# Transposes through the 128 rows of TensorE, or through its two 64-row halves: an RWKV-7 and SwiGLU kernel

## The chip, the core and the metric

The kernel runs on one core of a Trainium2 chip. The metric is the device time of one execution in microseconds (us), as the median of several runs. A profile of one execution tells what every engine did: TensorE (PE for matmuls, PEld for the loading of their stationary operand), VectorE (DVE), ScalarE (ACT), GpSimd (POOL) and SyncE (SP, which here only issues DMAs).

## What is computed

Two blocks follow each other. The first is a linear recurrence over 768 tokens for 4 x 8 heads of width 40, the second a feed-forward block on the 3072 rows of width 320 that the first one leaves.

```
for t in range(S):
    y[:, :, t] = einsum('bhd,bhde->bhe', r_t, state)
    Sa = einsum('bhde,bhe->bhd', state, a_t)
    state = state * w_t - outer(Sa, b_t) + outer(v_t, k_t)
...
x  = y as (batch*token, head*width)            # 3072 x 320
xn = x / sqrt(mean(x*x) + 1e-6) * g
out = (silu(xn @ w_gate) * (xn @ w_val)) @ w_out   # d_ff 1536
```

All data are fp32.

## The kernel before

**Tiling.** The 768 tokens are cut into 24 chunks of C = 32. The 32 pairs of batch and head lie as n (8), i (2, the half of 64 partitions in which the pair's tokens lie) and o (2, one of two heads that stand side by side). `front(c)` (L654) loads a chunk's inputs, transposes them, and builds the products of the decays and the triangular matrices by levels 4, 8 and 16; `inverse(c)` (L762; `early_inverse`, L780, for the first four) inverts a unit triangular matrix by 31 steps on VectorE; `main(c)` (L812) carries the state over the chunk and makes y; after each second chunk `feed(g)` (L941) runs the feed-forward block on 256 rows, in 12 slices of d_ff. The fronts run two chunks ahead of the mains.

**Natural tiles.** DMAs bring inputs with the tokens on partitions: a tile such as `wan` is [128, 8, 2, 64], where rows 0 to 63 belong to i = 0 and rows 64 to 127 to i = 1, and each head's 40 values stand in a slot of 64. Most matmuls need the head's width on partitions, so the kernel transposes such tiles on TensorE with an identity as the moving operand. All of these go through `flip` (L490, L491). One step of `plan` is a burst of flips, all into one room of PSUM:

- `turned` (L632 to L636) makes 8 flips, one for each n. In the front: `wan` (w and a, L670) and `kbn` (k and b, L684) with 128 rows and 104 columns of weights and 128 moving columns; `K` (L758) with 104 rows, 128 columns and 104 moving columns. In the main: `rn` (r, each second chunk, L847), `VU` (L856, out to `vut`) and the state `ST` (L860, out to `Sd`, 104 rows, 104 columns, 104 moving).
- `turn4` (L921) transposes y by 4 flips of 128 x 128, `turn3` (L932) the normalised x by 3.

After each burst ScalarE copies the room into SBUF: `T`, `A` and `Ab` (L678 to L682) from that of `wan`, `K` (L684), `KN` (L758), `rE` and `r2` (L849 to L852), `vut` (L856), `Sd` (L859); the Square and the scaling of `x` read that of y (L924, L927), and `xg` is made from that of x on ScalarE (chunks 0 to 5, L937) or VectorE (L939).

**Matmul shapes.** A matmul is told here by weights (rows x columns) and moving columns. The feed-forward block uses the whole array, 128*128, except for the last 64 rows of its 320 inputs: `h64` (L959) runs pairs with 64*128 weights, one in each half of the rows and each into another PSUM bank. The recurrence uses small ones: `gramk` (L693, L716) 40*64, `score` (L863) 40*64, `level` (L884) 128*40, `state`, `lower` and `update` 40*32, 32*32 and 64*40, and `y0` (L902) 40*40. Each fp32 matmul stands in the trace as two records, each transpose as one.

**Order.** Nothing is ordered by dependence at run time: `ORDER` (L33 to L228) lists all 6028 steps in the order in which they are issued, over all engines, each number counted from the first step that has not been issued; each "-" (151 of them) is a matmul on the identity that fills time (`plan.warm`, L1017). An engine works through its own steps in that order and waits by semaphores. PSUM is three rooms of two banks (`plan.pairs`, L439) and `po` for the feed-forward output; `PAIRS` (L230) says which of the three each step's output gets, and a room is held until its last reader is through.

Of the kernel before, what the change touches and what calls it, by code (L numbers as in the profile page):

```python
# [17 lines left out]
P = 128  # L18
C = 32
# [14 lines left out]
85 84 76 83 58 78 73 86 74 59 60 75 5 89 61 88 53 77 80 4 43 6 201 7 87 90 44 8 334 62 9 - - - - - - - - 93 10 18 79  # L34
11 12 214 557 13 213 567 14 15 94 566 210 16 17 95 558 108 200 - - - 97 96 19 335 20 21 2 209 22 23 98 25 199 568 26
100 578 202 24 101 107 569 111 57 - - - - - 102 106 124 589 27 122 112 392 109 103 52 119 113 104 54 577 155 125 110
204 105 120 - - - - - - 114 203 117 121 559 211 598 118 46 131 129 132 45 562 560 212 597 563 588 561 394 123 115 136
586 384 133 134 - - - - - 126 130 116 47 564 3 145 383 135 336 128 137 48 144 143 141 587 219 142 51 570 127 565 146
138 337 55 573 1005 216 579 281 393 220 582 608 571 390 234 379 239 607 572 583 580 380 251 574 222 38 221 609 575 581
42 - - - - - - - - 223 82 226 339 91 64 227 338 39 81 139 224 263 576 238 153 56 249 247 590 206 584 228 382 237 591  # L40
272 593 40 233 232 585 381 154 148 594 33 140 205 229 592 389 235 250 28 248 - - 325 236 32 245 36 230 147 260 282 391
246 259 150 35 34 326 595 0 36 270 155 214 148 242 243 62 605 598 230 - 239 40 616 599 601 628 64 49 91 600 602 30 48
626 1135 28 257 603 29 241 68 150 255 65 0 1347 194 0 194 84 173 0 - - - 182 540 200 0 557 184 1 186 935 542 540 0 506
515 527 257 513 300 0 111 97 110 61 112 96 51 439 458 122 50 243 480 0 244 0 58 255 242 0 259 709 104 120 246 708 247
456 470 258 488 719 0 256 470 457 242 0 716 265 487 104 0 268 0 0 265 473 0 262 277 0 273 0 236 0 260 0 269 0 461 241
- - - - - - - 237 242 0 0 278 242 243 252 0 252 0 0 89 0 99 246 0 97 0 230 94 440 0 230 94 440 231 - - - - - - - - -
240 441 244 0 0 468 440 451 255 0 42 468 269 469 258 215 440 239 204 0 0 257 253 203 93 449 92 212 0 235 - - - - - - -
- 246 0 437 0 262 0 246 247 436 245 464 470 258 259 469 260 244 - - 255 471 465 468 466 0 215 466 269 256 445 697 255
478 686 93 94 264 95 687 270 96 266 97 0 97 470 695 2 98 99 3 100 471 101 473 1 102 0 468 99 470 100 471 101 441 102
103 258 104 105 260 106 - - - - - - - - - - - 0 504 106 107 473 108 0 108 502 0 108 109 469 110 111 0 0 0 0 0 - - 13 0  # L50
374 16 146 143 14 147 142 15 13 355 - - - 25 386 358 0 358 386 388 16 387 389 25 390 79 17 391 28 70 147 355 191 69
356 80 148 149 26 359 0 28 2 29 149 0 149 150 29 0 149 31 185 391 23 32 390 29 150 356 151 186 33 389 0 151 29 387 152
27 40 187 153 154 155 156 33 157 158 159 160 161 34 162 36 163 164 37 165 41 391 38 42 392 39 394 561 166 395 393 552
0 42 548 395 209 0 560 165 42 395 548 210 43 428 211 427 557 44 - - - 565 166 558 45 167 549 168 0 566 168 739 565 567
738 571 169 579 - - 45 728 572 0 124 139 0 535 682 0 535 545 140 578 536 141 0 547 545 546 543 578 0 558 554 567 0 519
- - - - - - 517 377 696 378 380 381 695 518 120 685 135 526 - - - - - - 522 686 379 527 382 136 530 383 554 529 121 -
- 141 540 123 523 565 539 122 537 142 125 538 124 524 - - - - 145 525 148 534 149 152 154 551 535 147 555 - - 157 146
550 536 150 155 151 556 165 552 564 153 160 691 164 161 692 0 161 689 162 165 1 0 546 676 0 506 41 554 42 556 43 420
507 995 555 44 996 45 563 509 421 432 436 435 422 437 433 571 508 441 434 444 46 572 829 442 0 572 442 585 838 573 577
0 838 45 445 577 46 828 587 573 589 446 575 47 598 48 601 11 846 588 574 443 613 597 836 0 11 443 370 599 0 584 595  # L60
607 367 478 34 568 - - 35 830 594 36 567 820 38 - 476 37 571 366 570 0 605 356 433 434 435 436 120 437 0 317 318 319
320 441 321 322 323 324 355 456 458 459 442 4 357 325 457 326 327 328 443 0 443 328 329 330 331 357 0 35 331 3 0 37
450 359 3 36 358 331 332 357 333 356 0 462 448 330 461 464 331 332 468 364 447 463 31 467 476 458 333 365 334 335 0
425 439 441 302 426 436 0 6 439 2 0 435 332 2 436 443 444 0 448 332 442 334 443 333 340 449 0 297 329 342 32 330 - 3
33 341 334 0 332 331 0 332 293 441 295 333 0 438 0 436 333 336 295 337 309 438 338 1 375 342 310 365 374 515 27 292 0
362 292 26 28 44 339 29 34 27 32 338 0 646 29 34 336 647 32 0 439 64 315 647 339 440 634 441 63 340 0 287 413 606 312
313 607 623 12 314 615 414 0 410 310 411 603 619 27 412 475 413 620 414 415 621 416 311 633 28 417 812 418 312 625 - -
- - 476 313 419 420 421 822 258 314 422 423 0 810 423 625 637 477 2 0 819 2 257 0 420 421 645 310 422 0 - - - - - 310
422 3 313 32 630 311 423 33 643 424 641 631 312 0 0 637 20 635 420 647 613 21 421 611 648 819 23 38 22 422 809 423 39
659 24 3 612 36 818 424 651 25 808 621 425 59 660 426 249 427 58 0 427 3 25 428 249 4 28 47 0 - 614 428 429 28 430 431  # L70
0 26 25 614 617 484 31 27 627 0 458 590 400 600 401 0 12 582 32 401 33 583 25 0 579 30 21 - - - - - - - - - 588 29 591
22 453 397 428 398 605 23 0 23 429 24 609 0 590 24 397 588 602 1 604 398 601 429 430 399 2 427 0 584 - - - - - - - - -
- - - - - 4 397 0 25 397 4 0 393 394 28 21 23 27 395 598 24 22 424 607 0 35 395 37 396 24 2 424 47 397 398 38 399 400
25 401 28 402 403 588 0 405 2 30 28 404 3 403 0 584 25 27 585 598 600 422 31 599 28 595 29 427 428 429 52 0 563 392
391 562 389 390 400 573 396 7 398 397 570 0 381 367 402 0 1 569 576 381 501 570 0 509 649 575 382 498 0 507 403 382
399 402 0 706 399 400 419 715 403 0 655 715 401 705 402 0 402 783 361 657 403 703 360 655 404 359 0 711 566 700 655
565 712 564 3 563 404 8 0 3 639 0 403 3 0 400 401 402 712 403 355 0 710 968 406 715 1134 712 978 711 724 1133 632 561
976 716 416 663 729 634 977 562 563 717 713 986 665 564 565 566 975 567 401 568 714 569 985 570 571 967 572 723 722 -
0 403 726 402 572 401 573 0 726 738 736 573 739 574 664 575 737 576 577 3 723 751 578 579 760 580 747 581 582 633 583
4 584 0 584 585 634 586 636 587 635 588 734 633 0 746 588 - - - - - 403 757 589 722 590 3 404 591 592 593 594 595 596  # L80
408 597 598 599 600 601 602 603 604 714 405 605 409 406 410 0 727 726 728 711 0 711 408 712 721 0 417 723 600 601 3
602 401 735 737 0 741 602 735 721 0 739 0 0 330 342 10 196 313 197 198 324 20 199 200 201 202 203 0 203 340 338 204
325 339 4 324 206 205 335 5 6 0 335 336 346 343 344 228 345 0 0 227 0 200 343 226 344 342 3 341 235 13 625 234 202 229
8 233 204 232 203 230 201 231 227 348 4 349 228 350 351 352 353 354 355 356 0 0 351 3 0 351 7 352 16 353 3 354 355 8
356 357 358 359 360 361 362 0 359 5 360 361 6 0 355 6 356 357 358 359 218 16 360 361 220 362 223 363 227 224 364 225
228 365 229 0 365 536 366 367 527 368 369 524 225 370 16 371 372 525 195 229 534 373 230 0 195 249 536 230 231 525 232
541 250 0 399 533 203 0 541 730 371 231 540 372 373 0 371 229 543 254 539 372 230 200 373 726 544 393 374 445 551 255
375 554 394 231 376 567 377 565 378 0 736 395 554 231 541 735 232 539 555 733 378 567 379 579 565 743 233 380 540 381
4 563 734 382 575 588 383 744 236 386 234 384 576 587 319 385 235 5 396 320 6 548 549 544 397 552 400 551 399 0 544
386 397 561 560 545 546 402 0 557 0 398 401 557 553 399 518 519 0 564 571 524 551 665 525 566 570 567 400 438 550 565  # L90
# [280 lines left out]
def kernel(  # L371
# [260 lines left out]
    def turned(t, at=lambda n: n, ins=P, outs=TOP):  # L632

        ps = plan.room().rearrange("p u f -> p (u f)").rearrange("p (n t) -> p n t", n=N)
        pe("turn", [flip(ps[0:outs, at(n), 0:ins], t[0:ins, n, 0:outs], ident[0:ins, 0:ins]) for n in range(N)])
        return ps  # L636
# [413 lines left out]
```

## Time and profile before

| | us |
|---|---|
| median of 3 runs | 1080.83 (1078.80 to 1081.73) |
| span of the profiled execution | 1078.2 |
| median of the runs less that span | 2.6 |
| VectorE busy | 834.2 (77%) |
| ScalarE busy | 462.2 (43%) |
| GpSimd busy | 309.0 (29%) |
| transposes, busy time by tile: wan, kbn, VU, K, ST, y, rn, x | 27.4, 26.3, 26.2, 23.0, 21.2, 15.3, 12.6, 12.5 |

The profiled execution's own time outside its span is not listed. The busy time of TensorE counts each record from its start to its modelled end, and records overlap, so that starts tell more than ends: how long a burst keeps the engine is read from its first start to the first start of the next burst.

### The profile page before, as it was taken

The page shows a single profiled execution, that of the slowest core. Times are in us where ns is not written, and L with a number is a line of the kernel's source. Part 1 is how long each engine was busy: PE and PEld are TensorE (multiplying, and loading weights), DVE is VectorE, ACT ScalarE, POOL GpSimd, SP SyncE. Part 2 cuts the span into 40 slices and gives each one's busy share as a digit, 9 for nine tenths or more (in the row PEclk, how much of TensorE's full clock was granted, in tenths as well). Part 3 has the DMA queues.
Part 4 walks back from the last instruction along what each step waited for, and adds up shares of the span by engine and source line. Part 5 has one row for each costly group of instructions (what it writes and reads, how often), then busy time and mean ns, then how long its engine had stood idle before and what let it go on. Part 6 is the DMA issues. An engine that isn't in the chain of part 4 may idle for free. (4 is left out here: it accounts for less than half of the span.)

```text
span 1078.2 us, 53465 instructions
## 1 busy us (share of the span) xinstructions
PE 1010.2 (94%) x23406; PEld 828.3 (77%) x23406; DVE 834.2 (77%) x2861; ACT 462.2 (43%) x1043; POOL 309.0 (29%) x554
## 2 busy tenths in 40 slices
PE   6767899999999999999999999998999999999998
PEld 6766778777888787877788778887777887887776
DVE  7887879876868888887897888887788889797420
ACT  6845756643543433532443434433344344342211
POOL 9714404120532223241331331331332331200000
PEclk9778999999999999999999999999999999999999
DMA  9965448766564364574465654665545553744242
GB/s 180 196 155 123 73 106 220 213 127 177 124 142 122 99 150 116 144 145 120 96 152 133 146 126 112 142 142 123 126 106 110 134 150 90 162 109 123 77 140 86
DMA packets 172456, 143.34 MB, mean 133 GB/s; under 512 B 125504, under 2 KB 143872, under 8 KB 172224
## 3 DMA queue, kind: packets, MB, share of 16 engines
q1 hardware_dynamic: 153856, 116.96, 42.4%
q0 software_dynamic: 16192, 22.64, 12.2%
q8 instruction: 184, 3.01, 1.2%
q10 hardware_dynamic: 2176, 0.33, 0.2%
q14 instruction: 48, 0.39, 0.1%
HBM read 123.86 MB, written 15.99 MB: 130 GB/s over the span
## 5 line engine op out<-in xcount | busy, mean ns | idle before, releaser
L488 PE MATMUL ps<-xg,wf 128*128 128x256 f32 (+1 forms) x1728 | 355.2, 392 | 4.7 <-DVE xg L446 1.1
L488 PEld LDWEIGHTS ps<-xg,wf 128*128 128x128 f32 (+1 forms) x1728 | 261.6, 189 | 60.4 <-issue 16.9
L488 PE MATMUL po<-wf,hT 128*128 128x320 f32 x576 | 180.1, 445 | 0.1
L446 DVE TENSOR_TENSOR tmp<-Yi,M 128x60 f32<-128x60 f32 (+24 forms) x620 | 129.5, 209 | 19.7 <-DMA M<-sB 6.9
L446 DVE TENSOR_TENSOR Yi<-Yi,tmp 128x60 f32<-128x60 f32 (+24 forms) x620 | 130.2, 210 | 12.7 <-DVE ss L446 0.2
L466 ACT ACTIVATE sg<-ps 128x256 f32<-128x256 f32 x144 | 52.4, 383 | 192.4 <-PE ps L488 182.7
L488 PEld LDWEIGHTS po<-wf,hT 128*128 128x128 f32 x576 | 102.6, 191 | 34.0 <-issue 1.7
L485 POOL DMA_DIRECT2D VU<-in_v_dram x92 | 53.6, 587 | 234.2 <-PE ps L488 157.0
L446 DVE TENSOR_TENSOR hT<-ps,sg 128x256 f32<-128x256 f32 x144 | 59.0, 419 | 62.4 <-ACT sg L466 55.9
L469 ACT COPY KN<-ps 128x640 f32<-128x640 f32 x96 | 66.2, 691 | 76.6 <-PE ps L491 27.9
L488 PEld LDWEIGHTS ps<-Ab,K 40*64 40x64 f32 x4608 | 78.3, 139 | 26.4 <-issue 8.5
L446 DVE TENSOR_TENSOR K<-K,T 128x512 f32<-128x512 f32 (+1 forms) x192 | 93.3, 495 | 4.2 <-ACT K L469 2.1
L488 PE MATMUL ps<-Ab,K 40*64 40x56 f32 x4608 | 88.0, 225 | 8.8 <-ACT K L469 3.7
L485 POOL DMA_DIRECT2D kbn<-in_b_dram x92 | 53.4, 584 | 147.9 <-PE ps L488 147.0
L446 DVE TENSOR_TENSOR As<-ps,msi 128x256 f32<-128x256 f32 (+1 forms) x186 | 79.2, 475 | 18.3 <-PE ps L488 17.4
L469 ACT COPY K<-K 128x256 f32<-128x256 f32 (+1 forms) x168 | 71.8, 443 | 41.3 <-PE ps L488 20.3
L488 PEld LDWEIGHTS ps<-As,KN 128*40 128x40 f32 x3072 | 64.6, 122 | 15.1 <-issue 9.7
L485 POOL DMA_DIRECT2D wn<-in_w_dram x92 | 51.6, 565 | 83.7 <-DVE KN L446 34.7
L485 POOL DMA_DIRECT2D kbn<-in_k_dram x92 | 53.5, 585 | 73.8 <-PE ps L488 73.5
L488 PE MATMUL ps<-As,KN 128*40 128x32 f32 x3072 | 71.1, 203 | 3.7 <-issue 2.7
L446 DVE TENSOR_TENSOR y<-y,ps 128x256 f32<-128x256 f32 x119 | 49.9, 419 | 19.7 <-PE ps L488 17.6
L446 DVE COPY_PREDICATED LT<-near,ps 128x384 f32<-128x384 uint32 (+2 forms) x72 | 52.3, 727 | 3.6 <-PE ps L488 1.9
(133 smaller groups left out, 1544.5 us busy)
## 6 DMA issues: line engine op xcount, KB each, us to landing
wf<-sW SPq DMA_DIRECT2D x144, 480.0 KB, 4.3
M<-sB SPq DMA_DIRECT2D x80, 128.0 KB, 3.8
rn<-in_r_dram SPq DMA_DIRECT2D x24, 160.0 KB, 4.5
sW<-ex SPq DMA_DIRECT2D x16, 240.0 KB, 4.3
out_dram<-o SPq DMA_DIRECT2D x48, 80.0 KB, 3.9
kbn<-in_k_dram POOLq DMA_DIRECT2D x92, 40.0 KB, 3.5
kbn<-in_b_dram POOLq DMA_DIRECT2D x92, 40.0 KB, 3.3
wan<-in_a_dram POOLq DMA_DIRECT2D x46, 80.0 KB, 4.7
```

Source lines behind the costliest of these rows:

```text
L446: plan.add("DVE", kind, lambda at: fn(at(o), *m(at)), [o], aps(*args))
L466: plan.add("ACT", "act", lambda at: nc.scalar.activation(at(o), at(a), f, **kw), [o] + aps(acc), [a])
L469: plan.add("ACT", "copy", lambda at: nc.scalar.copy(at(o), at(a)), [o], [a])
L485: plan.add(by, "dma", lambda at: queue.dma_start(out=o, in_=i), [o], [i])
L488: return o, lhsT, rhs, lambda at: nc.tensor.matmul(at(o), lhsT, rhs, start=start, stop=stop, skip_group_check=True)
```

## The change

Every transpose of 128 (or 104) rows becomes two of 64 (or 40) rows: one reads rows 0 to 63 and the identity's upper 64 x 64 block, the other rows 64 to 127 and the lower block. The first writes bank 0 of the room and the second bank 1. The two are issued next to each other, so that a burst of 8 becomes one of 16, that of y 8 and that of x 6. `K`, `ST` and y use only the 40 rows of each half that hold data, so their moving operand has 40 columns; the other four have 64. The readers' access patterns follow the new layout and cover the same elements; the copies of `A` and `Ab` are split in two by i. These are two more steps on ScalarE in each of the 24 fronts, each put right behind its sibling. Decoded, the new `ORDER` has the 6028 old steps and the 151 fillers in the old sequence, and the 48 new ones. `PAIRS` is unchanged.

```diff
-    def turned(t, at=lambda n: n, ins=P, outs=TOP):
-        ps = plan.room().rearrange("p u f -> p (u f)").rearrange("p (n t) -> p n t", n=N)
-        pe("turn", [flip(ps[0:outs, at(n), 0:ins], t[0:ins, n, 0:outs], ident[0:ins, 0:ins]) for n in range(N)])
+    def turned(t, at=lambda n: n, ins=64, outs=TOP):
+        ps = plan.room()[:, :, 0:N * ins].rearrange("p u (n t) -> p n u t", n=N)
+        row = lambda u: slice(u * 64, u * 64 + ins)
+        pe("turn", [flip(ps[0:outs, at(n), u], t[row(u), n, 0:outs], ident[row(u), row(u)]) for n in range(N) for u in range(2)])
         return ps
+    natural = lambda t: t.rearrange("p n o e -> p n (o e)")
...
-        a4 = ps[:, :, :, 1].rearrange("p n i t -> p (n i) t")
-        copy(A[:, :, :, 0:3], a4.rearrange("p n (g j) -> p n g j", j=4)[:, :, :, 1:4])
-        copy(Ab[:, :, 0:C].rearrange("p n (b h j) -> p n b h j", b=2, j=4)[:, :, :, :, 0], a4.rearrange("p n (h b j) -> p n b h j", b=2, j=4)[:, :, :, :, 0])
+        for i in range(2):
+            copy(A[:, i::2, :, 0:3], ps[:, :, i, 1].rearrange("p n (g j) -> p n g j", j=4)[:, :, :, 1:4])
+        for i in range(2):
+            copy(Ab[:, i::2, 0:C].rearrange("p n (b h j) -> p n b h j", b=2, j=4)[:, :, :, :, 0],
+                 ps[:, :, i, 1].rearrange("p n (h b j) -> p n b h j", b=2, j=4)[:, :, :, :, 0])
...
-             turned(K.rearrange("p (n i) x s -> p n (i x s)", i=2), ins=TOP, outs=P).rearrange("p n (o e) -> p n o e", o=2)[:, :, :, 0:D])
+        copy(z["KN"][32].rearrange("p (n o e) -> p n o e", n=N, o=2), turned(K.rearrange("p (n i) x s -> p n (i x s)", i=2), ins=D, outs=P))
...
-        copy(vut, turned(VU.rearrange("p n o e -> p n (o e)"), slot))
+        copy(vut.rearrange("p n (i t) -> p n i t", i=2), turned(natural(VU), slot))
...
-                 turned(ST_.tiles[(c + 1) % 2].rearrange("p n i d -> p n (i d)"), ins=TOP).rearrange(
-                     "p n (o e) -> p n o e", o=2)[:, :, :, 0:D])
+                 turned(natural(ST_.tiles[(c + 1) % 2]), ins=D))
...
-        xn = plan.room()[:, 0].rearrange("p (m c) -> p m c", m=4)
-        pe("turn4", [flip(xn[:, m], y.rearrange("p (m c) t -> p m (c t)", m=4)[:, m], ident) for m in range(4)])
-        xv = xn.rearrange("p m (o e) -> p o m e", o=2)[:, :, :, 0:D]
+        xv = plan.room()[:, :, 0:4 * D].rearrange("p o (m e) -> p o m e", m=4)
+        ym = y.rearrange("p (m c) t -> p m (c t)", m=4)
+        pe("turn4", [flip(xv[:, o, m], ym[part(o), m], ident[part(o), part(o)]) for m in range(4) for o in range(2)])
...
-        ps = plan.room()[:, 0, 0:KT * P].rearrange("p (k t) -> p k t", k=KT)
-        pe("turn3", [flip(ps[:, kt, :], x[:, kt * P:(kt + 1) * P], ident) for kt in range(KT)])
+        ps = plan.room()[:, :, 0:KT * 64].rearrange("p u (k t) -> p k u t", k=KT)
+        pe("turn3", [flip(ps[:, kt, u], x[half(u), kt * P:(kt + 1) * P], ident[half(u), half(u)]) for kt in range(KT) for u in range(2)])
```

## The prediction, made before the changed kernel ran

> **What bounds the kernel.** I read the page's sums and slices first, then the timeline of TensorE in one chunk of the steady part, then the waits.
>
> ```profile
> span 1078.2 us, 53465 instructions
> PE 1010.2 (94%) x23406; PEld 828.3 (77%) x23406; DVE 834.2 (77%) x2861; ACT 462.2 (43%) x1043; POOL 309.0 (29%) x554
> ...
> PE   6767899999999999999999999998999999999998
> ...
> PEclk9778999999999999999999999999999999999999
> DMA  9965448766564364574465654665545553744242
> ```
>
> TensorE is full from about 110 us on at full granted clock. Before that it is 7 tenths busy and the DMA row stands at 9 and 6: there the loads and the first inverse set the time, and I count no gain there. From 110 us to the end I set TensorE's time together from the starts:
>
> ```profile
> 510.44 1.99 PE L488 MATMUL ps<-xg,wf 128*128 128x256 f32 x8
> 512.36 1.42 PE L488 MATMUL ps<-As,KN 128*40 128x32 f32 x64
> 513.71 0.93 PE L491 MATMUL ps<-ident,K 104*128 104x104 f32 x8
> 514.48 2.34 PE L488 MATMUL po<-wf,hT 128*128 128x320 f32 x8
> 516.65 1.04 PE L491 MATMUL ps<-ident,wan 128*104 128x128 f32 x8
> 517.62 0.78 PE L488 MATMUL ps<-ST,aP 40*32 40x40 f32 x64
> 518.40 1.13 PE L488 MATMUL ps<-xg,wf 64*128 64x256 f32 x8
> 519.46 0.79 PE L488 MATMUL ps<-VU,LT 32*32 32x40 f32 x64
> 520.18 3.72 PE L488 MATMUL ps<-xg,wf 128*128 128x256 f32 x16
> ```
>
> The first column is the start, so differences tell how long a burst holds the engine. Four things stand here.
>
> *Streaming.* Inside bursts of full-array records the trace's starts are 269 ns apart for 320 moving columns, 216 for 256, 109 for 128 (transposes of wan, kbn, VU, rn, y, x) and 89 for 104 (K, ST): 0.833 ns a column and 2.5 ns.
>
> *Halves run together.* The 8 records of 64*128 at 518.40 are done with in 1.06 us. One after another they would take 8 x 216 = 1.73 us; in the trace each pair starts 7 ns apart and the next pair 216 ns later. These pairs have just the rows, columns and two banks that the new transposes have.
>
> *Weights.* Bursts whose streaming is short are paced by weight loads. 128*40 (level, all rows) starts every 19.3 ns, so 40 columns cost 19.3. 40*64 (gramk) takes 59.4 ns for four, which lie in two row halves, two to each: 29.7 for 64 columns, if the halves load at the same time. The 64 records of 32*32 at 519.46 hold the engine 0.72 us, 11 ns each, which fits only if loads of different rows overlap. So 0.43 ns a column: 47 ns for 104 columns, 57 for 128.
>
> *Switching.* Where the shape of the array's tile changes from one burst to the next, 93 to 106 ns are added to the streaming (median of each kind, 64*128 to 128*128 being 93, and back 96); without a change 2 to 3. So wan before ST,aP holds the engine 0.97 us (872 + 96), K before po 0.77.
>
> **The change part by part.** From 110 us on the trace has 20 bursts of wan, 20 of kbn, 23 of VU, 11 of rn, 21 of K, 22 of ST, 23 of y and 24 of x.
>
> Transposes, each pair taking the longer of streaming and weights:
> - wan, kbn, VU, rn: 64 moving columns, 56 ns a pair; 8 pairs are 448 ns where 8 x 109 = 872 were. 74 x 424 ns = 31.4 us.
> - K: 40 columns (36 ns) under 128 columns of weights (57): 456 for 712. 21 x 256 = 5.4 us.
> - ST: 36 under 47: 376 for 712. 22 x 336 = 7.4 us.
> - y: 4 x 57 = 228 for 436. 23 x 208 = 4.8 us. x: 3 x 57 = 171 for 327. 24 x 156 = 3.7 us.
>
> Together 52.7 us of TensorE's time.
>
> No row shows a transpose on half the rows. Bounds: the pair at 36 to 57 ns by the h64 and gramk rows, or the two one after another (rival 1). For 128 columns of weights the trace bounds the load from above by 89 ns, the distance of K's transposes, which carry such weights (72 for 104 in proportion, rival 2). I take the lower values: the h64 row is the same tile shape.
>
> [...]
>
> Switches: transposes now have the h64 shape instead of the full array's. Of their neighbours in the kept order from 110 us on, 127 edges touch a full-array burst, each a new switch, and 20 edges touch h64, where one goes. 107 x 95 ns = 10.2 us lost. Edges to small tiles had a switch and keep it.
>
> ScalarE: two copies more per front. A takes 570 ns for 384 elements, Ab 398 for 128; a copy of 1024 takes 1012 and one of 640 692, so the fixed part is about 160 ns: 24 x 2 x 160 = 7.7 us. ScalarE idles 58% of 150 to 1000 us, mostly for TensorE, which hides it; uncovered it would be at most those 7.7. Other readers cover as many elements, and already alternate banks in KN (691 ns for 640), so nothing there. No DMA, room or filler moves. TensorE issues 1216 more weight loads and as many matmuls; at 28 ns a pair of instructions this is slower than the 9 to 15 ns of the small bursts, so it costs nothing.
>
> So TensorE's own sum falls by 52.7 - 10.2 = 42.5 us.
>
> **How much reaches the end.** TensorE hardly idles, but others come just in time:
>
> ```profile
> DVE hT L446 <- ACT sg L466: 32.8, 28, 5.7
> ...
> DVE y L446 <- PE ps L488: 28.6, 22, 5.7
> ...
> DVE As L446 <- PE ps L488: 16.9, 11, 5.1
> ...
> PE ps L488 <- issue: 13.6, 21, 1.8
> ```
>
> (150 to 1040 us: total, times, longest.) VectorE waits on TensorE and so moves up with it; it is 82% busy from 250 to 1000 us. But of 306 TensorE instructions that VectorE released last, 203 started within 200 ns of that. Following from the last instruction back to what let each start (its queue, if that allowed it within 30 ns, or the last semaphore), the chain leaves TensorE 41 times after 110 us, through VectorE, ScalarE and DMA waits. Only 607 of the 1100 transposes lie on it, and 69 of the 107 new switches: 23.5 us by the savings above. Counting only waits over 110 ns, 734 lie on it: 28.6 us. Ignoring all, 42.5. I take 27: nearer to the chain, since some of its short waits are lost records. What is late next is VectorE, and the POOL loads of k and b.
>
> 1078.2 - 27 = 1051 us of span; beside the median of the runs, 1080.8 - 27 = **1054 us**.
>
> **Rivals.**
> 1. *Halves don't overlap in transposes* (slower). If a transpose holds the array's path whatever its rows, 16 go one by one at the longer of 56 and the weights: 74 x 896, 21 x 912, 22 x 752, 23 x 456 and 24 x 342 ns are 7.8 us more than now, with the switches 18 us: 1099. It decides from 93 ns a pair: 113.0 us of transposes now, less 10.2, over 1100 pairs. For it: no transpose record of 64 rows. Against: h64 at 216 for a pair. If only the weight loads go one by one (94 and 114 ns a pair), it is 2.9 us saved and 10.2 lost: 1088. Against: the 11 ns of the 32*32 burst.
> 2. *Weights pace the pairs*, at 72 and 89 ns: 21.9 + 0 + 3.0 + 1.8 + 1.4 = 28.1, less 10.2 leaves 18, of which the same share reaches the end: 1069; slower loads still, up to 93 ns a pair, end at no change, 1080. [...] Against: the 19.3 and 29.7 ns.
> 3. *TensorE alone decides*, all 42.5 arrive: 1038. For: it idles 3% of 250 to 1000 us. Against: the just-in-time releases.
> 4. *It doesn't do what it says*: order, fillers and rooms are the old ones by the decoded lists, so little for this: 1080.
>
> **How the numbers follow.** Forecast 0.71 (1043 to 1066); rival 1 0.13 (0.10 at 1099, 0.03 at 1088); rival 2 0.08 (0.06 faster, 0.02 no change); rival 3 0.06; rival 4 0.02. 1036 to 1070 holds the forecast, rival 3 and most of rival 2, 0.8 in all. A measurement of this kernel tells some 0.3% from no change: faster 0.71 + 0.06 + 0.06 = 0.83, within 0.02 + 0.02 = 0.04, slower 0.13.
>
> **What the profile after would show.** Transpose records of 64*104 with 64 moving columns whose pairs start 7 ns apart and 56 ns after the last pair; K and y at 57, ST at 47. Some 93 ns at each edge to 128*128. More idle time of TensorE before bursts released by VectorE, and VectorE over 80% of the span. Pairs 93 ns apart or more would make the prediction wrong, and so would a TensorE whose waits grow by more than 25 us.

## The result, and the profile after

The changed kernel takes **1135.03 us** (median of 6 runs, 1123.65 to 1136.98); beside it, on the same chip, the kernel before takes 1081.22 (6 runs, 1074.67 to 1086.12). The ratio is **1.0486, with a 95% interval of 1.0433 to 1.0539**: 54 us slower, where 27 us faster was forecast. (Ratios compare undisturbed executions alone, and so can differ a little from the ratio of two medians; every profile used below is of an undisturbed execution but that of after_s128, which took 1.6% more than its fastest.) The profiled execution of after took 1128.14 us, its span is 1126.4, 48.2 more than before's 1078.2.

The sums and slices of the page of after, the counterpart of the first fence of the prediction:

```profile
span 1126.4 us, 55970 instructions
...
PE 1024.9 (91%) x24622; PEld 821.4 (73%) x24622; DVE 835.0 (74%) x2861; ACT 463.0 (41%) x1091; POOL 309.5 (27%) x554
...
PE   7779897899999999998998999999889998999998
...
PEclk8876798899889989989999999999989999999999
DMA  9964356756454364564455555545445544634342
```

The row PEclk is to be read first: it was 9 in every slice after the fourth, and now 8 stands again and again. The mean granted clock is 0.930, before's 0.980. By stretches of the trace of after (length, busy time of each engine with its instructions, then the granted clock, the share of the DMA engines and GB/s):

```profile
core 0: us, PE busy (x) PEld busy (x) DVE busy (x) ACT busy (x) POOL busy (x), PEclk, DMA share, GB/s
110.00:320.00 210.00, 187.82 (x4720) 151.75 (x4720) 147.94 (x485) 103.89 (x239) 57.21 (x97) 0.90 0.56 137
320.00:530.00 210.00, 197.11 (x4836) 154.74 (x4833) 169.31 (x600) 82.29 (x201) 55.21 (x94) 0.95 0.51 123
530.00:740.00 210.00, 196.51 (x4971) 156.62 (x4964) 168.90 (x601) 82.20 (x201) 61.31 (x105) 0.96 0.53 123
740.00:950.00 210.00, 191.08 (x4696) 150.72 (x4695) 162.84 (x578) 75.09 (x183) 60.81 (x104) 0.94 0.51 120
```

The same four stretches of before stand at 0.99 to 1.00. The work of TensorE itself got shorter, as forecast. This is the timeline of after where it issues the bursts that the prediction showed from 512.36 on:

```profile
537.89 1.42 PE L489 MATMUL ps<-As,KN 128*40 128x32 f32 x64
539.24 0.69 PE L492 MATMUL ps<-ident,K 40*128 40x40 f32 x16
539.86 2.42 PE L489 MATMUL po<-wf,hT 128*128 128x320 f32 x8
542.21 0.66 PE L492 MATMUL ps<-ident,wan 64*104 64x64 f32 x16
542.79 0.78 PE L489 MATMUL ps<-ST,aP 40*32 40x40 f32 x64
543.50 1.13 PE L489 MATMUL ps<-xg,wf 64*128 64x256 f32 x8
544.57 0.79 PE L489 MATMUL ps<-VU,LT 32*32 32x40 f32 x64
545.29 3.72 PE L489 MATMUL ps<-xg,wf 128*128 128x256 f32 x16
```

From the first start to the last it is 7.40 us, where it was 7.82. K holds the engine 0.62 us instead of 0.77, wan 0.58 instead of 0.97; the 320-column burst between them holds it 2.35 instead of 2.17, and has a switch behind it now. The prediction's terms give 0.256 + 0.424 - 2 x 0.095 = 0.49 us for this stretch, and 0.42 came.

What came on top is in the waits of TensorE from 150 to 1040 us (total, times, longest), of which the first was 13.6, 21, 1.8 before:

```profile
PE ps L489 <- issue: 38.8, 38, 5.0
PE ps L492 <- issue: 3.8, 3, 1.7
```

VectorE's waits in the same window, by contrast, are nearly those of before (32.8, 28.6 and 16.9):

```profile
DVE hT L447 <- ACT sg L467: 31.2, 36, 4.7
DVE y L447 <- PE ps L489: 27.9, 22, 6.7
DVE As L447 <- PE ps L489: 19.9, 11, 5.4
```

"issue" is an engine that waited for no other engine and no transfer that the profile shows. One such place, in the timeline of after, TensorE alone (the helper's line, then shape, number and, in brackets, the idle time before):

```profile
609.02 0.58 PE L492 MATMUL ps<-ident,ST 40*104 40x40 f32 x16
609.53 0.34 PE L489 MATMUL ps<-Ab,K 40*64 40x56 f32 x8
610.68 1.04 PE L489 MATMUL ps<-Ab,K 40*64 40x56 f32 x56 [0.81 <-issue]
...
612.15 0.31 PE L489 MATMUL ps<-rE,vut 40*64 40x32 f32 x7
615.79 1.72 PE L489 MATMUL ps<-rE,vut 40*64 40x32 f32 x56 [3.33 <-issue]
617.44 4.82 PE L489 MATMUL ps<-xg,wf 64*128 64x256 f32 x16
```

Two bursts are cut in two, one after 8 records of 64, with no wait for another engine or a transfer named. And the same place in windows of 3.4 us:

```profile
607.40:610.90 3.50, 2.69 (x58) 1.91 (x59) 2.53 (x11) 1.26 (x2) 1.63 (x3) 1.00 0.77 203
610.90:614.30 3.40, 1.56 (x128) 1.45 (x120) 0.50 (x2) 0.72 (x2) 0.00 (x0) 1.00 0.80 244
614.30:617.70 3.40, 1.91 (x58) 1.84 (x60) 0.05 (x1) 0.00 (x0) 0.00 (x0) 0.50 0.10 17
617.70:621.10 3.40, 3.40 (x12) 2.31 (x13) 3.30 (x9) 0.00 (x0) 0.00 (x0) 0.50 0.13 22
```

Behind the window with the idle time the clock (third number from the end) falls to one half for 6.8 us, and the pairs of 64x256 that start at 617.44 follow each other every 426 ns instead of 216 (from 621.1 on it is 216 again). VectorE, ScalarE and GpSimd run dry, too.

**What the cuts in the bursts are.** The pages list a DMA queue of the kind `instruction` whose packets grow with the number of TensorE's instructions. Its line on the pages of before and of after (packets, MB, share):

```profile
q8 instruction: 184, 3.01, 1.2%
```

```profile
q8 instruction: 193, 3.16, 1.2%
```

3.01 MB over 184 packets is 16 KB each; TensorE's instructions in the trace (2 x 23406 records and 327 on semaphores or draining) over 256 are 184.1 and, after, 2 x 24622 and 325 over 256 are 193.6. So I take a packet as 256 of TensorE's instructions, 64 bytes each: an estimate from these counts, which the places of the waits bear out. Numbered in the order of their starts, those on semaphores included, the instructions ahead of which TensorE stands on issue for over 0.7 us (after 110 us) have the numbers 193 or 194 modulo 256 in all 16 cases of before and in 30 of the 31 of after. In after they end 0.9 to 1.9 us after a packet has landed (for the wait that ends at 615.79 the packet ran from 613.38 to 614.38); the starts of two packets are never closer than 3.31 us in before and 3.35 in after, and only one in ten lies closer than 3.64. Where TensorE waited at such a limit in after, the 256 instructions ahead had been used up in 2.8 us (median), and the next ones came 4.5 us (median; 3.4 to 7.7) after these had begun. I call 256 such instructions a block.

The trace also shows what went ahead of these waits. In each of these 30 cases the packet that ended the wait started only after TensorE had begun the block ahead, 0.5 to 4.9 us after (1.9 in the median); it took 1.0 us, and the next block began 1.4 us after it had landed (medians). (Of the 192 packets of after that have a block ahead, 14 started earlier than that block, by up to 2.6 us.) The waits go with blocks that were used up fast: in after 37 of 175 blocks were used up within 3.5 us, and 22 of them were followed by such a wait, against 8 of the other 138.

**What the half clock follows.** In the traces of before and after the granted clock stands at 1 or 0.5 and nothing else, and its 13 and 45 changes lie whole multiples of 3.413 us apart, to 1.1 ns. I cut the time into windows on this grid and added, for each window at full clock after 100 us, the records' rows x columns x streaming time as a share of the full array (the window's array work). In before 3 of 283 windows are followed by half a clock, and these have the lowest work of all (0 where the program ends, 0.17 and 0.21; the lowest of the others is 0.27). In after 17 of 268 are, the program's end among them; of the 17 windows under 0.30, 16 are, and none over 0.32. In all 18 traces of this document together, with each record counted for the part of it that lies in the window, half a clock follows 110 of 114 windows under 0.20, 95 of 164 from 0.20 to 0.30, 18 of 266 from 0.30 to 0.40 and none of the 4407 above. So half a clock goes with little work, but the limit is not sharp, and what is counted is not settled: the plain share of the window in which anything streams, whatever its rows and columns, parts these windows as well (75 of 4951 on the wrong side of its best limit, 80 by the work). Halves lower both (a pair of VU follows the last after 56 ns, where a whole flip took 109). TensorE was not idle through all of such windows: the one ahead of 614.3 above, in which TensorE is at work for 1.56 of 3.40 us, on small tiles, is followed by half a clock as well.

### The profile page after: what moved, and what is told of

The parts are those of the page before. It is cut to its first block, busy times and chain, and to the rows that moved or that the text cites. A ratio compares the mean times of both kernels' runs of the same rounds, so it can differ in the third digit from the quotient of the medians.

```text
span 1126.4 us, 55970 instructions
## 1 busy us (share of the span) xinstructions
PE 1024.9 (91%) x24622; PEld 821.4 (73%) x24622; DVE 835.0 (74%) x2861; ACT 463.0 (41%) x1091; POOL 309.5 (27%) x554
## 3 DMA queue, kind: packets, MB, share of 16 engines
q1 hardware_dynamic: 153856, 116.96, 40.3%
## 4 chain that ended last, share of the span: by engine, by line
PE 60%; DVE 14%; issue 8%; DMA 8%; ACT 4%; POOL 3%; SPq 2%; DVEq 0%; ACTq 0%; POOLq 0%
PE ps L489 44%; PE po L489 11%; PE ps L492 4%; SPq L486 2%; DVE tmp L447 2%; DVE LT L447 2%; DVE Yi L447 2%; DVE y L447 2%; POOL kbn L486 1%; DVE K L447 1%; PE po L1022 1%; DMA kbn<-in_b_dram 1%; DMA M<-sB 1%; DMA kbn<-in_k_dram 1%; DMA LT<-sY 1%
## 5 line engine op out<-in xcount | busy, mean ns | idle before, releaser
L489 PE MATMUL ps<-xg,wf 128*128 128x256 f32 (+1 forms) x1728 | 371.0, 408 | 8.6 <-issue 3.8
L489 PEld LDWEIGHTS ps<-xg,wf 128*128 128x128 f32 (+1 forms) x1728 | 271.1, 198 | 68.9 <-issue 20.1
L489 PE MATMUL po<-wf,hT 128*128 128x320 f32 x576 | 191.6, 466 | 0.8 <-DVE hT L447 0.7
L489 PEld LDWEIGHTS po<-wf,hT 128*128 128x128 f32 x576 | 105.8, 197 | 39.0 <-issue 4.8
L489 PE MATMUL ps<-Ab,K 40*64 40x56 f32 x4608 | 92.1, 230 | 20.6 <-issue 12.3
L489 PEld LDWEIGHTS ps<-Ab,K 40*64 40x64 f32 x4608 | 81.7, 143 | 37.7 <-issue 19.9
L489 PEld LDWEIGHTS ps<-As,KN 128*40 128x40 f32 x3072 | 68.5, 127 | 17.3 <-issue 12.6
L489 PE MATMUL ps<-As,KN 128*40 128x32 f32 x3072 | 75.0, 208 | 5.9 <-issue 5.2
L447 DVE TENSOR_TENSOR y<-y,ps 128x256 f32<-128x256 f32 x119 | 49.9, 419 | 24.6 <-PE ps L489 22.5
L1022 PE MATMUL po<-ident 128*128 128x128 f32 x302 | 54.8, 342 | 3.3 <-DVE po L520 3.3
```

What stands on the lines that cost most here:

```text
L447: plan.add("DVE", kind, lambda at: fn(at(o), *m(at)), [o], aps(*args))
L489: return o, lhsT, rhs, lambda at: nc.tensor.matmul(at(o), lhsT, rhs, start=start, stop=stop, skip_group_check=True)
L1022: plan.warm = lambda: nc.tensor.matmul(po_[:, 0, DM:DM + P], ident, ident, start=False, stop=False, skip_group_check=True)
```

## The experiments

All of them are built from one frame, in which each burst of transposes can be whole, as before, or in halves, as changed; everything else (the two copies more per front among it) is that of the changed kernel. Three theories stood against each other at first: that the added instructions outrun the *supply* of instructions; that halves give the array less *work*, so that the clock falls; and that the *switches* between tile shapes cost more than priced.

**whole: the changed kernel with every transpose whole again.**

```diff
-        ps = plan.room()[:, :, 0:N * ins].rearrange("p u (n t) -> p n u t", n=N)
-        pe("turn", [flip(ps[0:outs, at(n), u], t[row(u), n, 0:outs], ident[row(u), row(u)]) for n in range(N) for u in range(2)])
+        ps = plan.room().rearrange("p u f -> p (u f)").rearrange("p (n t) -> p n t", n=N)
+        pe("turn", [flip(ps[0:outs, at(n), 0:span], t[0:span, n, 0:outs], ident[0:span, 0:span]) for n in range(N)])
```

> All transposes whole again in the changed kernel's frame; only the copies of A and Ab stay split in two. Every theory that puts the loss on the halves expects the time of the kernel before, 1076 to 1086 us, TensorE's idle time that ends in 'issue' at 20 to 28 us and a mean granted clock of 0.98. If the split copies cost, 1086 to 1090.

Measured: 1084.26 us beside 1084.11, ratio 1.0036 [0.9989, 1.0083], clock 0.978. The 48 copies more of ScalarE cost nothing that can be measured. All of the 54 us comes from the halving of the transposes and what goes with it: the added instructions and the layout in two banks. Of these the layout shows no price: ScalarE's busy time after, 463.0 us, is that of before, 462.2.

**nops: whole, with two instructions that do nothing behind each flip.**

```diff
+        more += [(o, i, j, lambda at: nc.tensor.nop(nofuse=True))] * (2 * len(steps))
```

> Whole transposes, and behind each flip two instructions on TensorE's queue that do nothing (16 in a burst of 8): as many instructions as the changed kernel, with the array work and the burst lengths of the kernel before. Theory A (TensorE's instructions come in blocks of 256, and a block that is used up in less time than its successor takes to come leaves TensorE idle; the granted clock then falls because of that idle time): idle time on issue 30 to 45 us, clock 0.94 to 0.97, 1095 to 1130 us. Theory B (the clock falls because halved transposes put less work on the array, whatever the number of instructions): 1078 to 1088 us, clock 0.98, idle time on issue as before.

Measured: 1078.05 us, ratio 0.9932 [0.9893, 0.9972]. It tells nothing on the supply: the profiled execution has 53515 instructions, exactly those of whole, and q8 brings 184 packets in both, so the added ones are not in it. As a second run of whole it shows that equal programs lie up to 1% apart, so that a difference of this size between two kernels here means little.

**one: only the halves of rows 0 to 63.**

```diff
-    ... for n in range(N) for u in range(2)])
+    ... for n in range(N) for u in range(1)])
+    return ps[:, :, 0:1].to_broadcast((P, N, 2, ins))
```

> Of each pair only the flip of rows 0 to 63 is issued, and the readers take it for both halves (so half the batch's data is left out of every transpose): as many instructions as before, bursts about as short as in the changed kernel, and a quarter of the array work. Theory A: idle time on issue 22 to 32 us, clock 0.95 to 0.98, 1045 to 1080 us. Theory B: at least the loss of the changed kernel, clock 0.93 or less, 1120 us or more.

Measured: 1108.47 us, ratio 1.0205 [1.0102, 1.0309], clock 0.923. It lies between the two expectations. It has as many matmuls and weight loads as whole and 63 fewer instructions on semaphores (53452 in all), and still is 24 us slower, with less for TensorE to do. So added instructions are not needed for a loss. The 63 go one by one over the whole length, so the limits between its blocks are not quite those of whole, but drift by up to 63 places. The rows of its page (the first) and of its waits (the second):

```profile
PEclk8575789999899989989997998999989999999999
```

```profile
PE ps L489 <- issue: 26.3, 35, 3.3
```

Waits on issue are little more than whole's (18.8, 27, 2.4 in the same line), and the clock falls all the same.

**one_nops: one, with the instructions that do nothing.** The edit is that of nops.

> As the run before with only the flips of rows 0 to 63, and two instructions that do nothing behind each flip, so that the number of instructions is that of the changed kernel. Theory A: back to the changed kernel's loss, 1115 to 1140 us, idle time on issue 40 to 55 us, clock 0.92 to 0.94. Theory B: the same time as with the flips of rows 0 to 63 alone, to 1%.

Measured: 1100.85 us, ratio 1.0173 [1.0094, 1.0251], clock 0.933. Again the added instructions are not among the profiled ones (53452, as in one), so it is a second run of one and confirms that.

**extra: whole, with a matmul of one column ahead of every second flip.**

```diff
+        one = lambda n: [mm(ps[0:outs, at(n), 0:1], t[0:span, n, 0:outs], ident[0:span, 0:1])] if n % 2 == 0 else []
-        pe("turn", [flip(...) for n in range(N)])
+        pe("turn", [s for n in range(N) for s in one(n) + [flip(...)]])
```

> All transposes whole, and ahead of every second flip one fp32 matmul with the same weights and a single moving column, whose output the flip writes over: 16 records more in a burst of 8, about the 2432 of the changed kernel, while their weight loads (47 ns each, 4 in 218 ns) fit under the flips' streaming. Theory A (the number of instructions runs TensorE dry, and that idle time lets the clock fall): gaps on issue 28 to 40 where the kernel before has 23, half-clock time over 80 us, 1092 to 1125 us. Theory B (array work in a window of 3.4 us decides the clock): half-clock time 40 to 60 us as before, 1078 to 1092 us.

Measured: 1185.27 us beside 1074.31, ratio 1.1033 [1.0971, 1.1095]. A miss of the design: the added instructions do not hide. Two flips with one such matmul ahead of them hold the engine 109 + 28 + 92 + 132 = 361 ns instead of 218, which for 608 of them is 87 us; whether their weight loads cost this or the turn from a matmul to a transpose is not shown. That slowed the use of instructions, and the waits on issue stayed small (21.1 us in the table below). It does not tell the theories apart.

**fill: the changed kernel with one matmul of the full array (two records of 128 columns) behind each burst.** The fillers of before and of after, the same matmul, start their records 112 ns apart at full clock (median).

```diff
+        more.append((o, i, j, lambda at: plan.warm()))
```

> The changed kernel with one full-array matmul on the identity (two records of 128 columns, 213 ns) behind each burst of transposes: 38 us more of TensorE's time, of pure array work. Theory B: half-clock time falls from 157 us to 60 to 90 us and gives back about what the fillers cost, 1105 to 1130 us. Theory A alone: the gaps on issue stay, half-clock time above 120 us, 1140 to 1165 us.

Measured: 1162.07 us, ratio 1.0806 [1.0743, 1.0869]. This is the range of theory A. Neither waits on issue nor half a clock went away (41.5 and 97.4 us after 110 us, where after has 48.0 and 105.8). More work placed behind the transposes does not fill the windows in which the work is low.

**calm and risky: halves in some of the bursts only.** In calm 78 bursts with busy surroundings are in halves, in risky 83 of the others.

```diff
+    HALF = lambda kind, c: c in {"wan": [...], "kbn": [...], ...}.get(kind, ())
```

> Halves in only 78 of the 179 bursts: those after 110 us around which, in the trace of before, every stretch of 3.4 us has at least 0.55 of the array's full work, and whose saving outweighs their new switches; by the rows 20 us of TensorE's time less. Theory B: clock 0.97 to 0.98, 1062 to 1076 us, faster than before. If the switches or the number of instructions make the loss instead: 1080 to 1100 us.

Measured: 1103.28 us, ratio 1.0270 [1.0211, 1.0329], clock 0.956.

> The opposite choice: halves in 83 bursts after 110 us around which some stretch of 3.4 us has less than 0.55 of the array's full work; these stand mostly between bursts of small tiles, so few switches are added, and the rows give 22 us of TensorE's time less. Theory B: half-clock time over 100 us, clock 0.93 to 0.955, 1090 to 1120 us. If the switches made the loss, this is the better choice: below 1070 us.

Measured: 1120.64 us, ratio 1.0441 [1.0378, 1.0505], clock 0.949. The theory of the switches falls here: after 110 us calm has 71 changes of the tile's shape more than whole and risky 39 (the changed kernel 103), and risky is the slower one. But calm, which should have lost next to nothing by the theory of the work, loses 29 us. Its waits on issue (36.4 us after 110 us) are more than twice whole's, with 44% of the added instructions, and those in calm places. That led to a sharper form of the supply theory: not how many instructions, but *which ones share a block*. Each added instruction moves all limits between blocks behind it, if these lie every 256 instructions, as the waits of before and of after do.

**whole_s64 and whole_s128: whole, with 64 or 128 tiny instructions ahead of everything.** Each added matmul has one column and 32 rows; two records and two loads come of it (53579 instructions in whole_s64, 53515 in whole).

```diff
+        for _ in range(16):     # 32 for whole_s128
+            nc.tensor.matmul(po_[0:32, 0, DM:DM + 1], ident[0:32, 0:32], ident[0:32, 0:1], start=False, stop=False, skip_group_check=True)
         plan.issue(ORDER, PAIRS)
```

> All transposes whole, and 16 tiny matmuls (64 records on TensorE, about 0.3 us) at the very start, where TensorE waits for the first loads: the same work in the same order, but every later instruction lies 64 places further on in the blocks of 256 in which TensorE's instructions arrive. Theory A' (what counts is which instructions share a block; the order of the kernel before happens to fit its blocks): after 110 us the idle time on issue goes from 15 to 30 us or more, half-clock time from 10 to 40 us or more, 1095 to 1125 us. Theory B (array work alone): 1074 to 1088 us, both as before.

Measured: **1138.01 us** beside 1079.86, ratio 1.0560 [1.0505, 1.0616], clock 0.952.

> The same with 32 tiny matmuls, 128 records, half a block. Theory A': idle time on issue and half-clock time differ from the run with 64 records and from none, at least one of the two shifts by more than 1.5% in time. Theory B: 1074 to 1088 us.

Measured: 1132.02 us, ratio 1.0500 [1.0454, 1.0546], clock 0.961. This decides it for the limits of the blocks: no transpose and no order is changed, and with 64 instructions more at the start the kernel is 54 us slower than whole, with 128 it is 48. The page of whole_s64 and, below it, its waits on issue:

```profile
span 1136.3 us, 53579 instructions
...
PEclk8887989999999999989999999999989999899999
```

```profile
PE ps L489 <- issue: 45.8, 39, 2.8
PE po L1055 <- issue: 3.8, 2, 1.9
```

30 of its 31 waits of over 0.7 us on issue lie again at 193 or 194 modulo 256, which now is other work. Of whole's 168 blocks after 110 us 20 are used up within 3.5 us, of whole_s64's 39: the same work, cut at other places, puts more of the fast stretches into one block.

**after_s64 and after_s128: the changed kernel with the same instructions ahead.**

> The changed kernel behind 64 records of tiny matmuls. Theory A': the time moves by 1% or more against the changed kernel without them, up or down, with the idle time on issue (48 us there) and the half-clock time (106 us). Theory B: 1123 to 1137 us, half-clock time 95 to 115 us.

Measured: 1139.06 us, ratio 1.0543 [1.0482, 1.0604], within 1% of the changed kernel's 1.0486.

> The changed kernel behind 128 records. Theory A': as with 64, another time; if the blocks made all of the loss, some shift would come below 1090 us. Theory B: 1123 to 1137 us.

Measured: 1127.48 us, ratio 1.0401 [1.0330, 1.0472], again within 1%. No position under 1090 was found. Four more runs followed.

**after_s192, after_s32 and whole_s192**: the same edit with 48, 8 and 48 of the tiny matmuls.

> The changed kernel with 192 tiny instructions (48 one-column matmuls and their loads) ahead of everything, so that every limit between blocks of 256 instructions falls 192 instructions earlier in the work: the last quarter of the circle after 0, 64 and 128. Theory of the blocks (the time is set by where the limits fall): any time from 1060 to 1150 us, and a time under 1090 would show that the halves pay once the limits fall well. Theory of the work (less array work in the transposes lets the granted clock fall whatever the limits do): 1125 to 1145 us, as with the other three positions.

Measured: 1144.13 us beside 1083.72, ratio 1.0548 [1.0492, 1.0604].

> The changed kernel with 32 tiny instructions ahead. Theory of the blocks: anything from 1060 to 1150 us; theory of the work: 1125 to 1145 us.

Measured: 1135.32 us, ratio 1.0477 [1.0417, 1.0537]. The changed kernel is 4.0 to 5.5% slower than before at all five positions tried; that some position of the limits would make the halves pay is not borne out by any of them.

> Whole transposes with the same 192 tiny instructions ahead. If the order of before fits only its own positions of the limits: 1115 to 1140 us, as at 64 and 128. If a limit that falls well is common: under 1095 us.

Measured: 1112.97 us, ratio 1.0263 [1.0206, 1.0320]. It lies between the two expectations, nearer to that of the special order: the old position is the best of the four tried for whole transposes (1084, 1138, 1132, 1113), and the others are not all alike.

**one_s64: one, with 64 tiny instructions ahead.**

> Only the halves of rows 0 to 63 (half of each transpose's data is left out, the number of instructions is that of before), with 64 tiny instructions ahead. At unmoved limits this kernel took 1108 us. If the loss to less array work (some 25 us there) and the loss to moved limits (some 50 us in the whole transposes) are separate and add: 1145 to 1165 us. If both are the same half-clock time, taken once: 1120 to 1140 us.

Measured: 1119.66 us, ratio 1.0337 [1.0290, 1.0383]. This is the edge of what one half-clock time, taken once, was to give. The losses do not add: moved limits cost whole transposes 54 us, and here 11. (The limits of one had drifted already, as told above, so that this is not a clean sum of the two.)

**The accounts.** For the profiled execution of each kernel, after 110 us: the idle time of TensorE on issue (what lies between two starts beyond the streaming and 110 ns, where it is over 250 ns), the time at half clock and its number of stretches (those that begin after 110 us, the one at the program's end among them), and what is left of the span without the first and without half of the second. At half clock the records of 256 columns start 427 ns apart and those of 320 columns 533, where it is 216 and 269 at full clock, so half a clock loses about half of its time at most, and some idle time lies inside it (0 to 7 us here), so the last column is an account, not a measurement.

| kernel | span | idle on issue | half clock | left |
|---|---|---|---|---|
| before | 1078.2 | 17.3 | 8.4 x3 | 1056.7 |
| whole | 1081.0 | 14.8 | 13.6 x4 | 1059.4 |
| nops | 1074.8 | 12.4 | 6.5 x3 | 1059.1 |
| whole_s64 | 1136.3 | 46.6 | 64.7 x15 | 1057.3 |
| whole_s128 | 1129.1 | 51.4 | 54.9 x14 | 1050.2 |
| whole_s192 | 1111.1 | 42.0 | 35.6 x8 | 1051.3 |
| after | 1126.4 | 48.0 | 105.8 x17 | 1025.5 |
| after_s32 | 1126.2 | 46.7 | 99.4 x16 | 1029.8 |
| after_s64 | 1138.5 | 49.9 | 104.3 x19 | 1036.4 |
| after_s128 | 1130.1 | 50.2 | 95.9 x16 | 1031.9 |
| after_s192 | 1142.1 | 57.6 | 119.1 x19 | 1024.9 |
| one | 1108.1 | 24.0 | 101.5 x15 | 1033.3 |
| one_nops | 1100.9 | 26.0 | 80.2 x14 | 1034.8 |
| one_s64 | 1117.7 | 29.4 | 118.6 x16 | 1029.0 |
| calm | 1108.2 | 36.4 | 49.9 x10 | 1046.9 |
| risky | 1112.9 | 40.3 | 83.2 x13 | 1031.0 |
| fill | 1161.8 | 41.5 | 97.4 x16 | 1071.6 |
| extra | 1185.5 | 21.1 | 58.2 x7 | 1135.3 |

The first six, with whole transposes, have 1050 to 1059 left, 1055.7 in the mean; the five of the changed kernel have 1025 to 1036, 1029.7 in the mean. So by this account the halves do save some 26 us of the path (24.5 if idle time inside half a clock is taken off once only), and the two losses outweigh it. From before to after: -31 of "left", +31 idle on issue, +49 half clock (half of 105.8 - 8.4), which is the 48 us of span.

Each of the two has its own cause, as far as the runs can part them. Idle time on issue is 42 to 58 us in the three shifted kernels with whole transposes and the five of the changed kernel, 36 to 42 in calm, risky and fill, whose limits have moved too, and 12 to 17 in before, whole and nops, whose limits lie as in before. The kernels of one half stand between (24 to 29). In extra, whose limits have moved as well but whose transposes take 87 us longer, it is 21. The time at half clock is 80 to 119 us in every kernel whose transposes are all in halves, even in one, with only 24 us idle on issue; with whole transposes it is 36 to 65 where the limits are moved, and 6 to 14 where not.

The fairest comparison is at moved limits on both sides, where the hand-written order no longer has the blocks it was written with. The three shifted kernels with whole transposes take 1.044 of before's time in the mean, the five with halves 1.049. Their means of idle time on issue are 46.7 and 50.5 us, of half clock 51.7 and 104.9, of "left" 1052.9 and 1029.7. So, as far as these means tell, nearly all of the added idle time on issue comes from limits that have moved, and little from the denser bursts; and the halves' saving of 23 us is paid back by 53 us more at half clock, 27 us if half of that is lost. What remains is most of the 54 us: the price of the moved limits, 29 to 54 us with whole transposes too (1113, 1132 and 1138, beside whole's 1084).

Window by window, both idle time on issue and smaller work can be seen ahead of half a clock as well. Of the 17 windows of after that are followed by half a clock, 13 have a fifth or more of their time idle on issue, 3 wait for other engines, and one is the program's end. If the transposes in them are counted at their whole size and all else is left, 6 of the 17 come from below 0.29 to that or more; the others stay low by their idle time. In one it is 4 of 15 with a fifth or more on issue, and 7 of 15 that the whole size would lift.

## Why the prediction was wrong

Step by step, as the prediction put them:

1. *Halves run together*, 56 ns a pair, K and y at 57, ST at 47, pairs 7 ns apart: **right**. At full clock the medians of after are 56 to 57 ns a pair for wan, kbn, VU and rn, 62 to 64 for K, y and x (a tenth over the 57) and 51 for ST, with the second half 3 to 7 ns behind the first. Rivals 1 and 2 fall.
2. *Switches at 93 to 106 ns*: **right in size**. A burst of VU holds the engine 586 ns up to the next burst, where it was 919 (medians): 333 saved, and 424 - 95 = 329 by the terms. Their number after 110 us rose by 103, where 107 were counted.
3. *ScalarE's copies hidden*: **right** (whole).
4. *27 of 42.5 us reach the end*: the size is **borne out**, as far as an account can: 26 us between the two groups of the table. TensorE's waits for other engines did grow, as foreseen, from 15.9 us after 110 us to 25.9.
5. *"TensorE issues 1216 more weight loads and as many matmuls; at 28 ns a pair of instructions this is slower than the 9 to 15 ns of the small bursts, so it costs nothing"*: **the step that failed**. By the account idle time on issue grew by 31 us, and half a clock cost more. The step compared with the pace inside one burst, and the waits stand at limits that lie 256 instructions apart: the packets of 256 start no closer than 3.31 us in before and 3.35 in after, and one in ten closer than 3.64, which is 13 to 14 ns for each instruction. A small burst uses its instructions far faster (128 of 32*32 in 0.72 us, 5.6 ns each); a whole transpose, two instructions in 89 to 109 ns, uses them at 45 to 55 ns each, slower than the packets bring them. A burst in halves issues 32 instructions in 0.45 us, 14 ns each: the pace of the packets at their closest, and no slower any more. That denser pace is the smaller part, by the account some 4 us of idle time. The larger is that every added instruction moves all later limits, against which the hand-written order of before, by chance or not, lies well: moving them by 64, with nothing else changed, costs 54 us.
6. *"Full granted clock"* **failed too**: it was read as a property of the kernel and carried over, and the time at half clock went from 8.4 to 105.8 us. Half a clock followed the windows of 3.41 us with the least work (in after 16 of the 17 under 0.30), and the change lowers that work twice: halves do the same transposes with half of the rows x columns x time (two of 64 rows in 56 ns, where one of 128 rows took 109), and idle time on issue, 48.0 us where it was 17.3, empties windows further.

The signs were there. The last of the shown waits, 13.6 us on issue in 21 places, was an engine that waited for nothing named, and was not followed up: all 16 waits on issue of over 0.7 us in before stand at a limit between blocks. The prediction did write that a TensorE whose waits grow by more than 25 us would make it wrong; they grew by 25.2 in just that line. No rival had supply or clock as its mechanism, and so the range missed.

**What stays open.** In one and one_s64 the smaller work, the 28 to 30 us of waits for other engines (16 in before) and the drifted limits stand together ahead of half a clock, and no run parts them. Whether the clock follows the work by rows and columns or the plain streaming time is not settled. Why the next block comes after 3.4 us in one place and after 7.7 in another is known only so far as that the packet starts late (0.5 to 4.9 us after the block ahead has begun); that time goes with the load on the DMA engines in the meantime only loosely (correlation about 0.5). A version faster than both kernels was not found. An order written anew for the halves, with their limits in view, was not tried; by the table it could win at most some 26 us.

## What to carry to other kernels

Count the instructions, not only the time: where a change replaces few long instructions by many short ones, add up the instructions in each 3.5 us and compare them with 256 (here 22 of the 37 blocks that were used up faster were followed by a wait of over 0.7 us, and 8 of the other 138), and look where the waits on "issue" lie in the profile before. This order, tuned by hand, turned out to be tuned to where its blocks end, too: 64 instructions ahead of it cost 54 us, more than the 26 us that the halves save by the account; shift the stream once by 64 instructions to learn how much of a difference is that. And a saving of array work in a kernel that lives at full clock must be checked against the windows with the least work, since half a clock followed these here (16 of the 17 windows under 0.30 in after).

## What the runs showed of the hardware that was not expected

- The packets of the instruction queue have 16 KB, 256 instructions of TensorE by the counts, and start 3.31 us apart at the closest; 30 of the 31 waits on issue of 0.7 to 5.0 us in after stand at the limits between such blocks, often in the middle of a burst, and in these 30 the packet started 0.5 to 4.9 us after the block ahead had begun.
- 64 instructions more at the start took a kernel from 1.004 to 1.056 of before's time.
- Half a clock for 3.41 us or a multiple followed windows of 3.41 us in which little streamed, by the measure of array work below about 0.3 of the full array, even with TensorE at work for part of them: 16 of 17 such windows in after, and 3 of 5 in before, where the two that were not followed by it stand at 0.27 and 0.28.
- A matmul of one column with 128 rows of weights between transposes costs 143 ns for two flips (361 instead of 218); why is not shown.
